# An attention, MLP and expert kernel: gated values on other engines, later routing sums, weights ahead of small tiles

## The chip, the cores and the metric

The kernel runs on one core of a Trainium2 chip. TensorE (PE in the profile) multiplies matrices, VectorE (DVE), ScalarE (ACT) and GpSimd (POOL) work element by element, SyncE (SP) issues most DMAs. Each engine runs its instructions in a fixed order and waits on semaphores for the others. The metric is the device time of one execution in microseconds (us); the kernel before took 972.35 us (median of three runs, 971.67 to 975.25).

## The reference, cut to what matters

```python
local = softmax(causal(q @ k.T / 8)) @ v               # 4 batches, 8 heads, 576 rows, 64 wide
mem   = (phi(q) @ M_prev) / (phi(q) @ z_prev + 1e-6)
x = g * mem + (1 - g) * local                          # 2304 tokens x 512
h = x @ w_in                                           # 512 -> 2048
x = (h * clip(h + 3, 0, 6) / 6) @ w_out                # 2048 -> 512
logits = x @ w_gate; e = argmax(logits)                # 8 experts, each token goes to one
out = p[e] * sigmoid((x @ w_output_gate)[e]) * (relu(x @ w1[e]) @ w2[e])
```

The MLP's output decides which expert each token goes to, so the expert stage starts with a sorting of the tokens ("routing") that can finish only when the MLP has.

## The kernel before, in words

Matrix products that need more precision than one pass gives are made of three: each operand is rounded to a shorter format (names ending in `H`) and the remainder is kept too (`L`), and HH, HL and LH products are added in PSUM.

**Attention** goes over 16 pairs of heads. For each pair, `scores` multiplies and VectorE takes the row minimum (`mn`, L343) while it copies the scores out of PSUM (`st`); `exp` on ScalarE gives `a`; `norm` on GpSimd divides by the sums (L365); `turn` transposes and `values` multiplies by v. A string of steps (`PROGRAM`) says in which order the steps of neighbouring pairs are written, and a scheduler then orders the instructions of each engine. Ahead of the first pair stand a few loads: q, k, the memory part's q (`qnt`), beta (`bt`), and the two gate matrices (`wg`, L409), which are rounded at once (`wgs`, L410 and L411) though they are used only after the MLP.

**The MLP** (`mlp`) works on blocks of 256 tokens and on two halves of the hidden width. In a block, each of eight units makes 128 hidden columns for 256 tokens (`hps`, L213), gates them (`g`, L216 on ScalarE and L217 on VectorE), rounds (`gH`, L95 on GpSimd) and takes the remainder (`gL`, L221 on GpSimd). The second product of a unit (`acc`, L182) is written two units later. After the second half's block, `end2` adds the first half's part (`row`, L528), makes the logits (`lg`) and, last, the gate factor (`gates`, L573 on).

Beside the last block, the expert that has most tokens so far is chosen, its weights are fetched (`st`) and split on ScalarE and VectorE (`wH` L641, `wL` L646), two tiles of its tokens are picked with one-hot matrices (`ohc`, L812) and gathered by GpSimd (`xg`, L659).

**The experts** take tiles of 128 tokens, 19 of them here. A tile is `hidden` (two halves of 512 columns, `ph`, 12 matmuls each), relu (`hs`, L693), transposes (`px`, L667), rounding and remainder (`hH`, `hL`), and `result` (`py`, L701, 24 matmuls). While a tile is computed, the weights of the next one are split again, and the ones after that are fetched chunk by chunk as `wL` frees a staging buffer. A fetch has a condition (`sw`): it moves no bytes where the next tile has the same expert. From here on the order of PE, DVE, ACT and POOL is as it is written (`manual_schedule`); SP's DMAs are ordered by the scheduler.

`route` writes the routing on VectorE in steps (`next(routing)`): counts, ranks and positions, one-hot matrices (`ohc`, `rh`), a product (`inv`, L908) that gives the token lists (`idx`), the expert of each tile and the condition (`ei`, `sw`, L901 and L902, from `c1` and `c2`), and last the lists of the small tiles (`inq`, `idq`, `esm`).

Four experts whose last tile has at most 32 tokens get no tile for them. These **small tiles** (`small`) run inside another tile, the host (tiles 4, 6, 9 and 11), one step after each of the host's groups of matmuls (`tick`): gather, transposes (`xT`), product (`ph`, L1038), relu (`hq`, L1043), transposes (`pt`, `hT`, L1047 and L1049), second product (`py`, L1056). Their weights (`sw` as a tile name: 8 chunks of 512 KB, L1020 and L1022) go through four buffers of their own. The expert numbers that SP needs for an address are read from `ei`, `sw` and `esm` by `value_load` (TENSOR_LOAD on SP).

Of the kernel before, what the change touches and what calls it, by code (L numbers as in the profile page):

```python
# [11 lines left out]
F32 = DT.float32  # L12
# [5 lines left out]
ALU = mybir.AluOpType  # L18
# [59 lines left out]
def f32(ap):  # L78
    return ap.bitcast(F32)
# [3 lines left out]
def tile_kernel(ctx, tc, qT, kT, qn, vx, z, beta, w_in, w_out, w_gates, w1, w2, out):  # L83
# [84 lines left out]
    def mlp(blocks, half_, end, begin=None):  # L168
# [24 lines left out]
        for n in blocks:  # L193
            xH = xs.tile([P, KD, TB], F32R, name="xH")
            xL = xs.tile([P, KD, TB], F32R, name="xL")
            o = n * TB % XB
            xn = xt[n * TB // XB][:, :, o : o + TB]
            for k in range(KD):
                copy(XH, xH[:, k], xn[:, k])
                ENG[XL].tensor_tensor(xL[:, k], xn[:, k], f32(xH[:, k]), op=ALU.subtract)  # L200
            if n == blocks[0]:
                yield
            if queue:
                second()
                follow()
                yield
            for m in range(HM):
                wH, wL = wts[half_][m]
                hps = ps_h.tile([P, 512], F32, name="hps", tag="h")[:, :TB]
                k = 0  # L210
                for kk in range(KD):
                    for ww, xx in ((wH, xH), (wH, xL), (wL, xH)):
                        PE.matmul(hps, lhsT=ww[:, kk * P : (kk + 1) * P], rhs=xx[:, kk], start=k == 0, stop=k == 3 * KD - 1)  # L213
                        k += 1
                g = gp.tile([P, TB], F32, name="g")
                ACT.activation(g, hps, AF.Relu, bias=half, scale=1.0 / 6.0)  # L216
                DVE.scalar_tensor_tensor(g, g, 1.0, hps, op0=ALU.min, op1=ALU.mult)  # L217
                gH = ghp.tile([P, TB], F32R, name="gH")
                gL = ghp.tile([P, TB], F32R, name="gL")
                copy(GH, gH, g)  # L220
                ENG[GL].tensor_tensor(gL, g, f32(gH), op=ALU.subtract)  # L221
                follow()
                yield
                if len(queue) >= (1 if m == 0 and n == NB - 1 else LAG):
                    second()
                    follow()
                    yield
                queue.append((n, m, gH, gL))
# [180 lines left out]
    SP.dma_start(wg, w_gates.rearrange("(k p) e -> p k e", p=P))  # L409
    ACT.copy(wgs[:, :, : 2 * E], wg)  # L410
    DVE.tensor_tensor(wgs[:, :, 2 * E :], wg, f32(wgs[:, :, : 2 * E]), op=ALU.subtract)  # L411
# [63 lines left out]
    for t in range(-1, len(pairs)):  # L475
        for x in PROGRAM.split():
            act(t, x)
    for _ in it:
        pass
# [266 lines left out]
    def flat(x):  # L746
        return x.rearrange("p a b -> p (a b)")
# [72 lines left out]
    def route():  # L820
# [16 lines left out]
        DVE.tensor_tensor(gtc, cnt.to_broadcast([P, E, NJ]), mid(io18, E), op=ALU.is_gt)  # L837
        yield
# [38 lines left out]

        c1, c2 = (r2.tile([P, NI, E], F32, name=x) for x in ("c1", "c2"))
        DVE.tensor_tensor(c1, mid(flat(base), NI), itl.to_broadcast([P, NI, E]), op=ALU.is_le)
        DVE.tensor_copy(tf, ti)  # L880
        DVE.tensor_tensor(c2, mid(flat(end), NI), itl.to_broadcast([P, NI, E]), op=ALU.is_le)
        gates = got["gates"]
        next(gates)
# [3 lines left out]
        DVE.tensor_tensor(c1, c1, c2, op=ALU.subtract)  # L887
# [3 lines left out]
        DVE.tensor_tensor(c1, c1, mid(io8, NI), op=ALU.mult)  # L891
# [4 lines left out]
        ef = r2.tile([P, NI + 1, 1], F32, name="ef")  # L896
        DVE.memset(ef[:, 0:1], 0.0)
        DVE.tensor_reduce(ef[:, 1 : NI + 1], c1, axis=AX.X, op=ALU.add)
        rh = r2.tile([P, NJ, 3, NI + NS], BF16, name="rh")
        DVE.tensor_tensor(rh[:, :, 0], mid(ion, NJ), tf.to_broadcast([P, NJ, NI + NS]), op=ALU.is_equal)  # L900
        DVE.tensor_copy(ei, flat(ef)[:, 1 : NI + 1])  # L901
        DVE.tensor_tensor(sw, flat(ef)[:, 1 : NI + 1], flat(ef)[:, 0:NI], op=ALU.not_equal)  # L902
# [12 lines left out]

        DVE.tensor_scalar(iv[:, 0], iv[:, 0], -1.0e6, 1.0e6, op0=ALU.mult, op1=ALU.add)
# [5 lines left out]
        DVE.tensor_copy(ivs, inv3[:, :, NI:])  # L922
        inq = ps_g.tile([P, 512], F32, name="inq", tag="pg")[:, : 3 * NS]
# [10 lines left out]
        c3 = r.tile([P, NS, E], F32, name="c3")  # L934
        DVE.tensor_tensor(c3, mid(flat(key), NS), ion[:, 1 : NS + 1].rearrange("p (n o) -> p n o", o=1).to_broadcast([P, NS, E]), op=ALU.is_equal)
        DVE.tensor_tensor(c3, c3, mid(io8, NS), op=ALU.mult)
        ef3 = r.tile([P, NS, 1], F32, name="ef3")
        DVE.tensor_reduce(ef3, c3, axis=AX.X, op=ALU.add)
        DVE.tensor_copy(esm, flat(ef3))
# [66 lines left out]
    def small(s):  # L1006
# [34 lines left out]
        yield  # L1041
        hq = smp.tile([P, FF // 4], F32, name="hq")
# [7 lines left out]
        for _ in range(9):  # L1050
            yield
# [26 lines left out]
    def tiles(i0, i1, w, xg, xn, xx):  # L1078
        nonlocal beside, smp
        for i in range(i0, i1):  # L1080
            if i + 1 in HOSTS and i + 1 < i1:
                ahead = small(HOSTS[i + 1])
                next(ahead)
# [7 lines left out]
            if more:  # L1091
                w.fetch(0, 1, 2, 3, 4, 5, 7, 6)
            high, low = (w.high, w.low) if more else (lambda *cs: None,) * 2

            hs, hh = hidden_out()
# [12 lines left out]
            ph = stepped(g, 2)  # L1108
            high(3)
# [110 lines left out]
```

## Time and profile before

| | |
|---|---|
| median of three runs | 972.35 us |
| the profiled execution | 975.48 us, of which the span from first to last instruction is 973.4 us |
| busy: PE, weight load, DVE, ACT, POOL | 94%, 74%, 64%, 53%, 38% of the span |
| mean granted TensorE clock | 0.978 of full speed |

The profile is of one execution. PE is the engine that is nearly always busy, so the time is read from the places where PE stands idle or runs at a lower clock, and from what ends each of those waits.

### The profile page before, as it was taken

To read this page: it belongs to the slowest core of one execution; us is meant where nothing else is said; L and a number is where in the kernel's file an instruction comes from. 1 tells how busy PE (TensorE), PEld (TensorE's weight loads), DVE (VectorE), ACT (ScalarE), POOL (GpSimd) and SP (SyncE) were. 2 spreads that over 40 slices of the span, in tenths; PEclk is the share of its full clock that TensorE was granted. 3 is DMA by queue.
4 is the path that set the end of the run, shared out by engine and by line. 5 is a ranking of instruction groups with operands and counts; after the bars stand their busy time and mean duration, and the time that the engine had idled before them with its cause. 6 is when DMAs were issued, how large, how long until landed. Compare 5 with 4: busy or idle time off the path is not lost. (4 is left out here: it accounts for less than half of the span.)

```text
span 973.4 us, 17053 instructions
## 1 busy us (share of the span) xinstructions
PE 915.6 (94%) x5733; PEld 721.7 (74%) x5733; DVE 627.7 (64%) x1511; ACT 519.3 (53%) x1084; POOL 370.5 (38%) x574
## 2 busy tenths in 40 slices
PE   5788889999999999899999999998997999999996
PEld 3445667777777778779988888887775777778785
DVE  6889996576556533686344444448766769668982
ACT  5677665565555454444222222223345768668883
POOL 2636556465555443245433333336021212112210
PEclk9989899999999999899999999999999999999998
DMA  5434432121212003443011111113223664633850
GB/s 181 139 112 146 131 100 74 52 86 52 78 54 90 14 23 109 130 131 108 1 45 44 44 44 45 44 44 138 80 77 120 218 250 176 208 131 119 311 205 23
DMA packets 49277, 101.69 MB, mean 104 GB/s; under 512 B 5341, under 2 KB 15581, under 8 KB 49184
## 3 DMA queue, kind: packets, MB, share of 16 engines
q1 hardware_dynamic: 45696, 89.74, 27.3%
q0 software_dynamic: 3488, 10.80, 3.3%
q8 instruction: 47, 0.77, 0.3%
q14 instruction: 46, 0.38, 0.1%
HBM read 136.66 MB, written 14.72 MB: 156 GB/s over the span
## 5 line engine op out<-in xcount | busy, mean ns | idle before, releaser
L646 DVE TENSOR_TENSOR wL<-st,wH 128x1024 fp32r<-128x1024 f32 x136 | 163.7, 1227 | 42.7 <-ACT wH L641 41.5
L95 POOL TENSOR_SCALAR gH<-g 128x256 fp32r<-128x256 f32 x144 | 65.5, 455 | 271.4 <-DVE g L217 213.5
L213 PE MATMUL hps<-xH,wH 128*128 128x256 f32 x576 | 167.3, 291 | 1.5 <-ACT xH L91 1.0
L213 PE MATMUL hps<-xL,wH 128*128 128x256 f32 x576 | 163.0, 283 | 2.4 <-DVE xL L200 2.4
L213 PE MATMUL hps<-xH,wL 128*128 128x256 f32 x576 | 161.7, 281 | 0.0
L365 POOL TENSOR_SCALAR a<-a,rs,omg 128x320 f32<-128x320 f32 (+4 forms) x160 | 128.1, 812 | 78.0 <-DVE rs L360 52.1
L217 DVE SCALAR_TENSOR_TENSOR g<-g,hps 128x256 f32<-128x256 f32 x144 | 60.0, 417 | 146.4 <-ACT g L216 146.4
L641 ACT CAST wH<-st 128x1024 fp32r<-128x1024 f32 x136 | 139.7, 1053 | 8.4 <-DMA st<-w 8.3
L216 ACT ACTIVATE g<-hps,half 128x256 f32<-128x256 f32 x144 | 68.1, 473 | 139.2 <-PE hps L213 116.0
L213 PEld LDWEIGHTS hps<-xH,wH 128*128 128x128 f32 x576 | 109.5, 191 | 18.3 <-issue 12.6
L221 POOL TENSOR_TENSOR gL<-g,gH 128x256 fp32r<-128x256 f32 x144 | 115.8, 804 | 11.7
L213 PEld LDWEIGHTS hps<-xL,wH 128*128 128x128 f32 x576 | 109.8, 191 | 8.4 <-DVE xL L200 3.4
L352 ACT ACTIVATE a<-st,mn 64x64 f32<-64x64 f32 (+4 forms) x160 | 88.4, 555 | 43.9 <-DVE mn L343 43.8
L213 PEld LDWEIGHTS hps<-xH,wL 128*128 128x128 f32 x576 | 109.8, 191 | 0.1
L182 PE MATMUL acc<-wH,gH 128*128 128x512 f32 x288 | 95.8, 414 | 0.2 <-POOL gH L95 0.2
L337 PE MATMUL pa<-kd,qd 64*128 64x64 f32 (+5 forms) x384 | 82.1, 470 | 13.8 <-DVE mn L343 8.7
L182 PE MATMUL acc<-wH,gL 128*128 128x512 f32 x288 | 91.6, 400 | 2.3 <-POOL gL L221 2.3
L182 PE MATMUL acc<-wL,gH 128*128 128x512 f32 x288 | 91.0, 398 | 0.0
L376 PE MATMUL pa<-ident,a 128*128 128x128 f32 (+1 forms) x480 | 75.3, 289 | 13.3 <-DVE mn L343 8.0
L376 PEld LDWEIGHTS pa<-ident,a 128*128 128x128 f32 (+1 forms) x480 | 55.6, 145 | 37.1 <-DVE mn L343 14.0
L708 POOL DMA_INDIRECT out<-ys,idxs x17 | 19.2, 1128 | 124.7 <-ACT ys L707 69.4
L182 PEld LDWEIGHTS acc<-wH,gL 128*128 128x128 f32 x288 | 54.3, 190 | 15.9 <-POOL gL L221 3.1
(239 smaller groups left out, 1720.8 us busy)
## 6 DMA issues: line engine op xcount, KB each, us to landing
st<-w SPq DMA_DIRECT2D x136, 512.0 KB
sw<-w SPq DMA_DIRECT2D x32, 512.0 KB
w<-w_in SPq DMA_DIRECT2D x16, 512.0 KB
w<-w_out SPq DMA_DIRECT2D x16, 512.0 KB
qnt<-qn SPq DMA_DIRECT2D x16, 320.0 KB
vt<-vx SPq DMA_DIRECT2D x16, 320.0 KB
x2d<-row SPq DMA_DIRECT2D x18, 258.0 KB
qd<-qT SPq DMA_DIRECT2D x16, 288.0 KB
```

The costliest lines, as they stand in the source:

```text
L95: POOL.tensor_scalar(out, x, 1.0, 1.0, op0=ALU.mult, op1=ALU.mult)
L182: PE.matmul(acc[t], lhsT=gg[:, t * P : (t + 1) * P], rhs=ww[:, 512:1024], start=m == 0 and first, stop=m == HM - 1 and last)
L213: PE.matmul(hps, lhsT=ww[:, kk * P : (kk + 1) * P], rhs=xx[:, kk], start=k == 0, stop=k == 3 * KD - 1)
L216: ACT.activation(g, hps, AF.Relu, bias=half, scale=1.0 / 6.0)
L217: DVE.scalar_tensor_tensor(g, g, 1.0, hps, op0=ALU.min, op1=ALU.mult)
L221: ENG[GL].tensor_tensor(gL, g, f32(gH), op=ALU.subtract)
L337: PE.matmul(pss[j][: QN[i], o : o + k1 - k0], lhsT=self.qd[r, QS[i] : QS[i] + QN[i]], rhs=self.kd[r, k0:k1], start=True, stop=True)
L352: ACT.activation(self.a[j][:m, o + D : o + D + n], self.st[j][i][:m, :n], AF.Exp, bias=self.mn[j][:m, i : i + 1], scale=-1.0, accum_out=se ...
L365: ENG[NORM[i]].tensor_scalar(av, av, r[:m, i], omg[:m, h : h + 1], op0=ALU.mult, op1=ALU.mult)
L376: PE.transpose(psa[:, off : off + QN[i]], self.a[j][: QN[i], QO[i] + c * P : QO[i] + (c + 1) * P], ident[: QN[i], : QN[i]])
L641: ACT.copy(self.H[c], stage[c])
L646: DVE.tensor_tensor(self.L[c], stage[c], f32(self.H[c]), op=ALU.subtract)
```

## The change

The change has six edits. In the MLP's last block of the second half, from the fourth unit on (`m >= 3`), `gH` is made on ScalarE and `gL` on VectorE. The load and split of `wg` are written after the attention loop. In `route`, the first step of `gates` comes earlier, the sums for `ei` and `sw` come after `idx`, and the sums for `esm` come before `inq` and end in a step of their own. In `small`, four steps are added before `hq` and three taken away after `hT`. In `tiles`, the small tile's first step (gather, `esm`, four fetches) comes after the next tile's weight fetch. In tile 2, two routing steps are written earlier than the tile's end.

```diff
+                near = half_ == 1 and n == NB - 1 and m >= 3
+                copy("A" if near else GH, gH, g)
+                ENG["D" if near else GL].tensor_tensor(gL, g, f32(gH), op=ALU.subtract)
...
-    SP.dma_start(wg, w_gates.rearrange("(k p) e -> p k e", p=P))
-    ACT.copy(wgs[:, :, : 2 * E], wg)
-    DVE.tensor_tensor(wgs[:, :, 2 * E :], wg, f32(wgs[:, :, : 2 * E]), op=ALU.subtract)
...
         for x in PROGRAM.split():
             act(t, x)
+    SP.dma_start(wg, w_gates.rearrange("(k p) e -> p k e", p=P))
+    ACT.copy(wgs[:, :, : 2 * E], wg)
+    DVE.tensor_tensor(wgs[:, :, 2 * E :], wg, f32(wgs[:, :, : 2 * E]), op=ALU.subtract)
...
         DVE.tensor_tensor(gtc, cnt.to_broadcast([P, E, NJ]), mid(io18, E), op=ALU.is_gt)
+        gates = got["gates"]
+        next(gates)
         yield
...
-        DVE.tensor_tensor(c1, mid(flat(base), NI), itl.to_broadcast([P, NI, E]), op=ALU.is_le)
         DVE.tensor_copy(tf, ti)
-        DVE.tensor_tensor(c2, mid(flat(end), NI), itl.to_broadcast([P, NI, E]), op=ALU.is_le)
-        gates = got["gates"]
-        next(gates)
         yield
...
         DVE.tensor_copy(idx, tok)
+        DVE.tensor_tensor(c1, mid(flat(base), NI), itl.to_broadcast([P, NI, E]), op=ALU.is_le)
+        DVE.tensor_tensor(c2, mid(flat(end), NI), itl.to_broadcast([P, NI, E]), op=ALU.is_le)
+        DVE.tensor_tensor(c1, c1, c2, op=ALU.subtract)
+        DVE.tensor_tensor(c1, c1, mid(io8, NI), op=ALU.mult)
+        ef = r2.tile([P, NI + 1, 1], F32, name="ef")
+        DVE.memset(ef[:, 0:1], 0.0)
+        DVE.tensor_reduce(ef[:, 1 : NI + 1], c1, axis=AX.X, op=ALU.add)
+        DVE.tensor_copy(ei, flat(ef)[:, 1 : NI + 1])
+        DVE.tensor_tensor(sw, flat(ef)[:, 1 : NI + 1], flat(ef)[:, 0:NI], op=ALU.not_equal)
...
         DVE.tensor_copy(ivs, inv3[:, :, NI:])
+        c3 = r.tile([P, NS, E], F32, name="c3")
...
+        DVE.tensor_copy(esm, flat(ef3))
+        yield
         inq = ps_g.tile([P, 512], F32, name="inq", tag="pg")[:, : 3 * NS]
...
         while len(ws) < 2 * KD:
             fetch()
         yield
+        for _ in range(4):
+            yield
         hq = smp.tile([P, FF // 4], F32, name="hq")
...
-        for _ in range(9):
+        for _ in range(6):
             yield
...
-            if i + 1 in HOSTS and i + 1 < i1:
-                ahead = small(HOSTS[i + 1])
-                next(ahead)
...
                 w.fetch(0, 1, 2, 3, 4, 5, 7, 6)
+            if i + 1 in HOSTS and i + 1 < i1:
+                ahead = small(HOSTS[i + 1])
+                next(ahead)
             high, low = (w.high, w.low) if more else (lambda *cs: None,) * 2
 
+            if i == 2:
+                next(routing)
...
             ph = stepped(g, 2)
+            if i == 2:
+                next(routing)
             high(3)
```

VectorE at the end of the MLP's last block, before (line numbers are those of the kernel before):

```order
L818 SCALAR_TENSOR_TENSOR id_5328<-iv_7789 128x1
L646 TENSOR_TENSOR wL_7917<-st,wH_7915 128x1024
L817 COPY iv_7835<-pi 128x2
L217 SCALAR_TENSOR_TENSOR g<-g,hps 128x256
L818 SCALAR_TENSOR_TENSOR id_5328<-iv_7835 128x1
L646 TENSOR_TENSOR wL_7921<-st,wH_7919 128x1024
L959 SCALAR_TENSOR_TENSOR esi_5337<-id_5328,esi 128x1
L646 TENSOR_TENSOR wL_7945<-st,wH_7943 128x1024
L217 SCALAR_TENSOR_TENSOR g<-g,hps 128x256
L646 TENSOR_TENSOR wL_7949<-st,wH_7947 128x1024
L672 TENSOR_TENSOR xgL<-px,xgH 128x512
```

The same place of the changed kernel, whose lines from here on stand two or more higher:

```order
L820 SCALAR_TENSOR_TENSOR id_5328<-iv_7789 128x1
L223 TENSOR_TENSOR gL<-g,gH 128x256
L217 SCALAR_TENSOR_TENSOR g<-g,hps 128x256
L819 COPY iv_7835<-pi 128x2
L648 TENSOR_TENSOR wL_7917<-st,wH_7915 128x1024
L820 SCALAR_TENSOR_TENSOR id_5328<-iv_7835 128x1
L223 TENSOR_TENSOR gL<-g,gH 128x256
L962 SCALAR_TENSOR_TENSOR esi_5337<-id_5328,esi 128x1
L648 TENSOR_TENSOR wL_7921<-st,wH_7919 128x1024
L217 SCALAR_TENSOR_TENSOR g<-g,hps 128x256
L648 TENSOR_TENSOR wL_7945<-st,wH_7943 128x1024
L223 TENSOR_TENSOR gL<-g,gH 128x256
```

Five remainders `gL` have come from GpSimd into VectorE's order; the last of them stands ahead of the last `wL`.

ScalarE in a host tile, before (`xT`, `hq` and `hT` are the small tile's):

```order
L707 ACTIVATE ys<-py,xg 128x512
L1033 COPY xT<-px 128x128
L1043 ACTIVATE hq<-ph 128x256
L1049 COPY hT<-pt 128x256
L641 CAST wH_8784<-st 128x1024
L641 CAST wH_8786<-st 128x1024
L693 ACTIVATE hs<-ph 128x512
L641 CAST wH_8793<-st 128x1024
```

The same place of the changed kernel:

```order
L709 ACTIVATE ys<-py,xg 128x512
L1036 COPY xT<-px 128x128
L643 CAST wH_8777<-st 128x1024
L643 CAST wH_8779<-st 128x1024
L695 ACTIVATE hs<-ph 128x512
L643 CAST wH_8786<-st 128x1024
L1048 ACTIVATE hq<-ph 128x256
L1112 CAST hH<-px 128x512
L1054 COPY hT<-pt 128x256
```

`hq` and `hT` have moved behind the host's relu `hs`.

SP's queue after the weight fetch of tile 3, before (`esm` is the small tile's expert, `sw<-w` its weights, `st<-w` a tile's weights):

```order
L636 DMA st<-w 128x2x512
L654 TENSOR_LOAD ei
L654 ISA x2
...
L1009 TENSOR_LOAD esm
L1009 ISA x2
L1020 ISA
L1020 DMA sw<-w 128x1024
...
L636 REGISTER_ALU x2
L636 ISA
L636 DMA st<-w 128x1024
```

The same place of the changed kernel, where tile 4's fetch ends and the small tile's begins:

```order
L638 DMA st<-w 128x2x512
L1012 TENSOR_LOAD esm
L1012 ISA x2
L1023 ISA
L1023 DMA sw<-w 128x1024
...
L656 TENSOR_LOAD ei
L656 ISA x2
L657 TENSOR_LOAD sw
L657 ISA x2
```

Before, eleven pairs of `ei` and `sw` loads, the wait for `esm` and the small tile's fetches stand ahead of tile 4's fetch; now that fetch stands ahead of them, and each tile's pair of loads stands right before its own fetch.

## Rows read from the trace of the kernel before

**Rows 1.** PE's waits, whole run: us in total, times, longest us

```profile
PE px L667 <- ACT hs L693: 7.7, 6, 3.8
```

**Rows 2.** Stretches: us, busy time of each engine, clock, DMA share, GB/s

```profile
676.00:686.00 10.00, 7.70 (x33) 6.08 (x32) 6.21 (x10) 3.35 (x5) 6.31 (x6) 0.83 0.69 254
710.00:720.00 10.00, 9.19 (x50) 7.04 (x50) 3.17 (x10) 1.94 (x4) 2.05 (x2) 0.83 0.24 67
720.00:735.00 15.00, 13.71 (x66) 10.80 (x66) 12.61 (x20) 11.16 (x14) 2.69 (x2) 1.00 0.12 36
735.00:755.00 20.00, 16.16 (x95) 11.77 (x94) 12.05 (x15) 11.25 (x15) 4.92 (x5) 0.91 0.44 156
800.00:820.00 20.00, 20.00 (x96) 16.14 (x95) 17.53 (x17) 17.95 (x25) 7.26 (x6) 1.00 0.65 239
```

**Rows 3.** Timeline of the start, ACT, DVE, PE: start us, us, instruction, idle before

```profile
9.23 0.24 ACT L410 CAST wgs<-wg 128x64 fp32r<-128x64 f32 x1 [2.68 <-DMA wg<-w_gates]
...
10.39 0.82 DVE L292 SCALAR_TENSOR_TENSOR phi<-qnt,phi 128x640 f32<-128x640 f32 x1
...
12.42 2.07 PE L337 MATMUL pa<-kd,qd 64*128 64x512 f32 x2 [4.63 <-DVE mn L343]
```

**Rows 4.** Timeline of the MLP's end, PE, POOL, DVE

```profile
681.50 1.22 PE L182 MATMUL acc<-wH,gL 128*128 128x512 f32 x2 [2.31 <-POOL gL L221]
685.39 0.39 PE L688 MATMUL ph<-wH,xgH 128*128 128x512 f32 x1
...
668.92 2.64 POOL L221 TENSOR_TENSOR gL<-g,gH 128x256 fp32r<-128x256 f32 x1
679.85 1.60 POOL L221 TENSOR_TENSOR gL<-g,gH 128x256 fp32r<-128x256 f32 x1
...
679.10 1.78 DVE L646 TENSOR_TENSOR wL<-st,wH 128x1024 fp32r<-128x1024 f32 x1
```

**Rows 5.** The page's costliest groups, VectorE's gate: busy us, mean ns | idle before

```profile
L217 DVE SCALAR_TENSOR_TENSOR g<-g,hps 128x256 f32<-128x256 f32 x144 | 60.0, 417 | 146.4 <-ACT g L216 146.4
```

**Rows 6.** Timeline of the routing, DVE, ACT, PE

```profile
703.79 0.35 DVE L879 TENSOR_TENSOR c<-base,itl 128x192 f32<-128x192 f32 x1
704.06 0.17 DVE L880 CAST tf<-ti 128x18 f32<-128x18 int32 x1
...
704.81 0.20 ACT L576 ACTIVATE so<-so 128x2 f32<-128x2 f32 x1 [8.00 <-DVE so L575]
...
710.81 0.85 PE L908 MATMUL inv<-rh,ohc 128*128 128x84 bf16 x18 [1.40 <-DVE rh L904]
```

**Rows 7.** Timeline of tile 3, PE, ACT, SP

```profile
733.47 0.17 PE L924 MATMUL inq<-ivs,four 128*128 128x12 bf16 x1 [1.29 <-DVE ivs L922]
741.77 0.66 PE L667 MATMUL px<-ident,hs 128*128 128x128 f32 x4 [3.84 <-ACT hs L693]
...
739.23 1.99 ACT L641 CAST wH<-st 128x1024 fp32r<-128x1024 f32 x2 [6.32 <-DMA st<-w]
...
736.64 2.08 SPq L1020 DMA_DIRECT2D sw<-w  x4
```

**Rows 8.** Timeline of host tile 6, PE; last row: ACT in host tile 4

```profile
789.72 0.39 PE L688 MATMUL ph<-wL,xgH 128*128 128x512 f32 x1
789.95 0.40 PE L688 MATMUL ph<-wH,xgL 128*128 128x512 f32 x1
791.11 0.66 PE L667 MATMUL px<-ident,hs 128*128 128x128 f32 x4 [0.76 <-ACT hs L693]
793.24 0.40 PE L701 MATMUL py<-wL,hH 128*128 128x512 f32 x1
793.91 0.50 PE L701 MATMUL py<-wH,hL 128*128 128x512 f32 x1 [0.28 <-DVE hL L1107]
...
755.02 0.39 ACT L1043 ACTIVATE hq<-ph 128x256 f32<-128x256 f32 x1 [2.30 <-PE ph L1038]
```

**Rows 9.** Stretch in which the first small tile's four fetches end

```profile
746.00:747.00 1.00, 1.00 (x8) 0.76 (x7) 0.80 (x1) 0.17 (x1) 0.00 (x0) 0.92 0.29 99
```

More of the change, by code (lines that the diff above doesn't have):

```diff
@@ L219, in mlp @@
                 gL = ghp.tile([P, TB], F32R, name="gL")
-                copy(GH, gH, g)
-                ENG[GL].tensor_tensor(gL, g, f32(gH), op=ALU.subtract)
+                near = half_ == 1 and n == NB - 1 and m >= 3
+                copy("A" if near else GH, gH, g)
+                ENG["D" if near else GL].tensor_tensor(gL, g, f32(gH), op=ALU.subtract)
                 follow()
@@ L876, in route @@
         DVE.tensor_copy(cf, ci)
-        c1, c2 = (r2.tile([P, NI, E], F32, name=x) for x in ("c1", "c2"))
-        DVE.tensor_tensor(c1, mid(flat(base), NI), itl.to_broadcast([P, NI, E]), op=ALU.is_le)
         DVE.tensor_copy(tf, ti)
-        DVE.tensor_tensor(c2, mid(flat(end), NI), itl.to_broadcast([P, NI, E]), op=ALU.is_le)
-        gates = got["gates"]
-        next(gates)
         yield
@@ L886, in route @@
         next(gates)
-        DVE.tensor_tensor(c1, c1, c2, op=ALU.subtract)
         next(gates)
@@ L890, in route @@
         next(gates)
-        DVE.tensor_tensor(c1, c1, mid(io8, NI), op=ALU.mult)
         next(gates)
@@ L895, in route @@
         yield
-        ef = r2.tile([P, NI + 1, 1], F32, name="ef")
-        DVE.memset(ef[:, 0:1], 0.0)
-        DVE.tensor_reduce(ef[:, 1 : NI + 1], c1, axis=AX.X, op=ALU.add)
         rh = r2.tile([P, NJ, 3, NI + NS], BF16, name="rh")
         DVE.tensor_tensor(rh[:, :, 0], mid(ion, NJ), tf.to_broadcast([P, NJ, NI + NS]), op=ALU.is_equal)
-        DVE.tensor_copy(ei, flat(ef)[:, 1 : NI + 1])
-        DVE.tensor_tensor(sw, flat(ef)[:, 1 : NI + 1], flat(ef)[:, 0:NI], op=ALU.not_equal)
         DVE.tensor_scalar(rh[:, :, 1], rh[:, :, 0], iop, None, op0=ALU.mult)
@@ L914, in route @@
         DVE.tensor_copy(idx, tok)
+        c1, c2 = (r2.tile([P, NI, E], F32, name=x) for x in ("c1", "c2"))
+        DVE.tensor_tensor(c1, mid(flat(base), NI), itl.to_broadcast([P, NI, E]), op=ALU.is_le)
[7 more added lines that the diff above has]
+        DVE.tensor_tensor(sw, flat(ef)[:, 1 : NI + 1], flat(ef)[:, 0:NI], op=ALU.not_equal)
         DVE.tensor_scalar(iv[:, 0], iv[:, 0], -1.0e6, 1.0e6, op0=ALU.mult, op1=ALU.add)
@@ L922, in route @@
         DVE.tensor_copy(ivs, inv3[:, :, NI:])
+        c3 = r.tile([P, NS, E], F32, name="c3")
+        DVE.tensor_tensor(c3, mid(flat(key), NS), ion[:, 1 : NS + 1].rearrange("p (n o) -> p n o", o=1).to_broadcast([P, NS, E]), op=ALU.is_equal)
+        DVE.tensor_tensor(c3, c3, mid(io8, NS), op=ALU.mult)
+        ef3 = r.tile([P, NS, 1], F32, name="ef3")
+        DVE.tensor_reduce(ef3, c3, axis=AX.X, op=ALU.add)
+        DVE.tensor_copy(esm, flat(ef3))
+        yield
         inq = ps_g.tile([P, 512], F32, name="inq", tag="pg")[:, : 3 * NS]
@@ L933, in route @@
         DVE.tensor_copy(idq, tks)
[L934 to L939, printed above, removed]
         yield
```

## The prediction

> **What bounds the kernel now.** I read the table of waits of PE first, because PE is busy for 94% of the span, then the table by stretches, then the timeline of each place where PE waits. The longest class of waits after the start is for the relu `hs`: 7.7 us in 6 waits, one of them 3.8 [rows 1]. The stretches [rows 2] show where PE has work to win back: in 800 to 820 it is busy for all of the 20.00 us at full clock, so an ordinary expert tile has nothing to give; in 676 to 686, 710 to 720 and 735 to 755 it is idle for 2.3, 0.8 and 3.8 us, and the mean clock is 0.83, 0.83 and 0.91. The clock has two levels (1.2 and 2.4 GHz), so 0.83 over 10 us is 3.4 us at the lower one and 0.91 over 20 us is 3.6 us; half of that is lost, 1.7, 1.7 and 1.8 us. So each of those waits costs more than its length. The start has one more long wait, 4.63 us [rows 3]. What the change can give is the sum over these places; all else is covered by a full PE.
>
> **The start.** ScalarE stands 2.68 us for the DMA of `wg` [rows 3], in front of the exponentials that VectorE needs, and VectorE's score minima, which free PE's banks, stand behind its part of `wgs`; PE's 4.63 us wait ends with them. With `wg` gone from here, ScalarE's next operand is `bt`, issued before `wg`; when it lands the trace does not show, only that ScalarE went on with it right after the `wgs` cast that starts at 9.23. So the gain is 2.7 at most and 0 at least; a loss would need ScalarE to be held longer by the fetches that now come earlier (`w_out` is cast before the first pair's exponentials end). The new order also puts `phi` (0.82 us) ahead of the first minimum, which cost nothing while it stood behind it. From 2.7 less 0.8 I take **1.8 us**. It is kept to the end if the attention's engines only wait for each other and nothing for a fixed time; the moved `wgs` pieces, 0.24 us each, then lie beside a full PE.
>
> **The MLP's last block.** PE waits 2.31 us for the remainder `gL`, which started late on GpSimd and took 1.60 us there; another took 2.64 us [rows 4]. With the lower clock after it that is 4.0 us. On ScalarE and VectorE neither wait exists for `gL`, but VectorE has no idle time here until its last weight remainder ends at 679.10 + 1.78 = 680.9 [rows 4], and five `gL` come on top. The trace shows none of this operation on VectorE; the gate of the same shape takes 0.42 us [rows 5], so five take 2.1. The first tile's `hidden` then waits for `xgL` behind that last remainder: 680.9 + 2.1 = 683.0, less some 0.4 that GpSimd no longer takes from VectorE by an estimate from the 1.78 us, against a start at 685.39 [rows 4]. That is 2.4 to 3.4 us; bounds are 0 (VectorE is the new limit all the way to the routing) and 4.0. I take **2.9 us**. The trace bears on this from another side: the remainder of 2.64 us on GpSimd ran while VectorE built its one-hot matrix. The Trainium skill ("SBUF — State Buffer", section "Who interferes with whom") says that a VectorE instruction with two SBUF inputs and a GpSimd one that reads SBUF exclude each other for a whole instruction, and the trace agrees with its 2.64. By that rule the five remainders on VectorE could still push back GpSimd's gather of the first tile, by up to 2.1 us, and the sum below would be 15.0 instead of 17.1.
>
> **The routing.** From the last `oh` to `inv` VectorE works without a break, and PE waits 1.40 us for it before `inv` [rows 6]. Four `c` sums leave that chain at 0.27 each (703.79 to 704.06 [rows 6]), and with the reduction and two casts for `ei` and `sw`, which I estimate at 0.4 from the same rows, 1.5 us. Against that, the first `gates` step now stands ahead of `hH` in ScalarE's order: `hH` and `hL` wait until VectorE has made `so`, some 0.8 us by the steps between. In return the output and the relu behind it no longer wait for `so` (8.00 us of ScalarE [rows 6]); that is PE time which the `inv` wait would take back. Net **0.65 us**, with -1.0 and 1.5 as ends. The 1.7 us of lower clock around 715 go or stay: the waits that remain before `inv`, about 1.9 us, lie between those that brought it (2.5 with the two ahead of it) and the 1.29 us before `inq`, after which the clock is 1.00 [rows 2, 7]. If they go, VectorE's sums for `ei`, now behind `idx`, delay the next `hL` by 0.8. Of 0 to 0.9 I take **0.4**. The Trainium skill ("TensorE: Matmul & The Clock Gate", Part 1) calls the slow clock the default that activity releases; by that rule any wait left here could bring it back, this term would be 0, and the sum 16.7.
>
> **Tile 3.** PE waits 1.29 us at `inq`, because `ivs` came after all weight remainders of tile 2, and 3.84 us for `hs`; ScalarE was held 6.32 us by the fetch of tile 4's weights [rows 7]. That fetch moves next to nothing: it stood in SP's queue behind the small tile's four fetches, which SP issued at 736.64 when `esm` was made, and ScalarE went on at 739.23. Now `ivs` and `esm` come at the start of tile 2, where VectorE waits, and the tile's fetch stands first, so both waits end: 1.3 + 3.8 + 1.8 of clock = 6.9. The seven small operations from `iq` to `idq` now stand inside tile 2 ahead of a weight remainder and `hL`; they come in all to about 1.4 us, of which half finds VectorE idle. **6.2 us**; ends are 0 and 6.9. The `ei` and `sw` loads now wait for sums behind `idx` and come some 3 us later, but SP has the rest of tile 1 for them.
>
> **The hosts.** `hq` waits 2.30 us for the small product on ScalarE [rows 8], and the host's own casts and `hs` stand behind it. PE pays 0.76 and 0.28 us in each host. From start to start it is 1.16 (789.95 to 791.11) and 0.67 (793.24 to 793.91), where matmuls without a wait stand 0.23 apart (789.72 to 789.95) [rows 8]: 1.83 - 0.46 = 1.4. Now `hq` comes behind `hs` and has its input by then, and `hT` waits for `pt` about 0.7 us in front of one cast that has as much slack. I take 1.3 each, four times: **5.2 us**, with 0 and 5.6 as ends.
>
> **The sum.** 1.8 + 2.9 + 0.65 + 0.4 + 6.2 + 5.2 = 17.15 us. The profiled execution took 975.48 us, so it would take 958.3. It was 3.1 us slower than the median of the runs, 972.35; from the median the sum gives 955.2, and I forecast **955**.
>
> **Rivals.** (1) *Tile 3's wait stays.* SP reaches tile 4's fetch late for another reason, such as the later `ei`; for it speaks that both loads now stand in the queue right before each fetch, against it that SP has 8 us and more. Without the 3.8 and 1.8 the time is 960.8. (2) *The early gains are not kept.* VectorE stays the limit from the MLP's end to the routing, and the start is absorbed by the attention. For it: VectorE's full order at the block's end. Without 1.8 and 2.9 it is 959.9. (3) *New waits in the old places.* The host tiles wait for `hT` instead of `hq`, the lower clock comes back in all three places, and the block's end stays. That gives back 5.2, 0.4, 1.8, 2.9 and, with `idq` in full in front of `hL`, 0.7 and the routing's 0.65: 966.9 at the start's full gain, some 968.5 without it. (4) *The small weights come late, and the kernel is slower.* Now the four fetches of a small tile stand behind the weights of the tile before its host. Before, they were issued at 736.64 and the traffic ended within 746 to 747 [rows 9], 10 us later. Now they can be issued when tile 3's last weight remainder frees its buffer, at the end of tile 2, about 734.5 on this time scale; they land by 744.5. PE needs them one tile of some 12.5 us (48 matmuls at 0.23, 12 transposes) and a few matmuls after 732, about 745.9. So there is 1.4 us to spare. If they were to land a further 10 us later, as behind eight fetches that really move bytes, each host waits 8.6 us, four of them 34, and the time is 989. The point from which this decides is 4.3 us of wait per host; tiles of the same expert, which move nothing, speak against it.
>
> **How the numbers follow.** The forecast has 0.66, rival 1 0.12, rival 2 0.14, rival 3 0.05, rival 4 0.03. What a measurement of this kernel can tell from no change is 0.5%, here 4.9 us, so faster means under 967.5. The forecast and rivals 1 and 2 lie there: 0.92. Rival 3 lies around that line: same, 0.05. Slower: 0.03. With the upper ends of all terms (2.7 + 4.0 + 1.5 + 0.9 + 6.9 + 5.6 = 21.6) the median is 950.8, and the start and the clock can be off by a little more; the range reaches from 948 to 964, so that it takes in rivals 1 and 2.
>
> **What would show it.** Right: no wait of `acc` for `gL` and a first `ph` about 3 us nearer to the last `hps`; no `inq` wait, no wait of ScalarE for `st` in tile 3, clock 1.00 there; no `px` wait for `hs` in the four hosts; PE's second group of scores about 2 us earlier. Wrong: PE waiting for `sw` in a host, `wH` still waiting for `st` in tile 3, or new waits of PE for `hL` in tiles 1 and 2 above 1 us. The forecast falls if two of the three terms above 2.5 us fail.

## The result and the profile after

The changed kernel took 960.42 us (median of four runs, 959.20 to 960.97) against 972.01 of the kernel before in the same comparison (four runs): ratio 0.9872, interval 0.9848 to 0.9895. A second comparison gave 960.66 against 973.28, ratio 0.9865 (0.9838 to 0.9893). By the medians the gain is 11.6 and 12.6 us; the forecast was 955, a gain of 17.15. The sign was right and about 5 us were missing.

The profiled execution after took 959.20 us, with a span of 957.3. First PE's stretches, at the places that answer to [rows 2] (columns as there):

```profile
671.00:681.00 10.00, 10.00 (x71) 8.44 (x70) 9.72 (x17) 5.96 (x11) 3.03 (x2) 1.00 0.64 237
...
704.00:714.00 10.00, 7.51 (x49) 5.53 (x49) 6.29 (x20) 1.22 (x3) 2.18 (x2) 1.00 0.34 108
714.00:729.00 15.00, 14.89 (x69) 11.06 (x68) 13.17 (x24) 12.58 (x17) 2.71 (x2) 1.00 0.12 36
729.00:749.00 20.00, 20.00 (x122) 15.12 (x121) 15.40 (x16) 15.48 (x22) 6.20 (x5) 1.00 0.68 244
```

The reader is to see that PE is now full in the MLP's last block (10.00 of 10.00, before 7.70; both stretches end just behind the first `ph`) and in tile 3 (20.00 of 20.00, before 16.16), in this execution all at full clock. Counted over the ten microseconds from the last `hps` on, the block has 9.56 where it had 7.70. Only the routing, 704 to 714, still has larger holes: 2.5 us idle. The table of PE's waits says the same. The class that was longest in the experts, `px` for `hs` [rows 1], has left its first twenty rows, and what is left from the last block on is small:

```profile
PE py L703 <- DVE hL L674: 1.4, 2, 0.8
...
PE inv L899 <- DVE rh L895: 1.1, 1, 1.1
...
PE pf L762 <- DVE ohb L824: 1.0, 1, 1.0
...
PE px L1034 <- DMA sx<-x2d,idr: 0.3, 1, 0.3
```

**The start**, timeline of ScalarE and PE, which answers to [rows 3]:

```profile
9.53 0.21 ACT L411 ACTIVATE gt<-bt 128x8 f32<-128x8 f32 x1 [3.38 <-DMA bt<-beta]
...
13.30 3.30 PE L339 MATMUL pa<-kd,qd 64*128 64x512 f32 x4 [5.37 <-DVE mn L345]
```

ScalarE's wait has only changed its name: it stands for `bt` now, to 9.53 instead of 9.23, and PE's long wait is 5.37 us instead of 4.63; its second group of scores starts at 13.30, before at 12.42.

**The MLP's end**, DVE, PE and ACT, which answers to [rows 4]:

```profile
678.23 0.42 DVE L223 TENSOR_TENSOR gL<-g,gH 128x256 fp32r<-128x256 f32 x1
678.56 1.22 DVE L648 TENSOR_TENSOR wL<-st,wH 128x1024 fp32r<-128x1024 f32 x1
...
679.73 0.40 PE L690 MATMUL ph<-wH,xgH 128*128 128x512 f32 x1
...
680.72 1.05 ACT L643 CAST wH<-st 128x1024 fp32r<-128x1024 f32 x1 [1.60 <-DMA st<-w]
...
684.79 1.05 ACT L643 CAST wH<-st 128x1024 fp32r<-128x1024 f32 x1 [0.70 <-DMA st<-w]
```

A remainder `gL` takes 0.42 us on VectorE, as the prediction bounded it from the gate's row, and no `acc` waits for it. The last weight remainder takes 1.22 us where it took 1.78. New are waits of ScalarE for the weights of the next tile, 1.60, 0.30 and 0.70 us. The kernel before had none behind its last `hps`.

**The routing**, ACT, DVE and PE, which answers to [rows 6]:

```profile
692.29 0.17 DVE L571 TENSOR_TENSOR oh<-t,mx 128x16 f32<-128x16 f32 x1
...
694.17 0.21 ACT L578 ACTIVATE so<-so 128x2 f32<-128x2 f32 x1 [2.33 <-DVE so L577]
694.28 0.57 ACT L673 CAST hH<-px 128x512 fp32r<-128x512 f32 x1
694.88 0.69 DVE L674 TENSOR_TENSOR hL<-px,hH 128x512 fp32r<-128x512 f32 x1 [0.74 <-ACT hH L673]
...
706.83 0.85 PE L899 MATMUL inv<-rh,ohc 128*128 128x84 bf16 x18 [1.07 <-DVE rh L895]
...
711.60 0.50 PE L703 MATMUL py<-wH,hL 128*128 128x512 f32 x1 [0.84 <-DVE hL L674]
```

`hH` is held behind `so`, VectorE waits 0.74 us for it, and `inv` is 14.54 us behind `oh`. In the trace before it was 14.74 (`oh` at 696.07).

**Tile 3**, PE and SP, which answers to [rows 7, 9]:

```profile
721.00 0.18 PE L933 MATMUL inq<-ivs,four 128*128 128x12 bf16 x1
...
730.46 2.10 SPq L1023 DMA_DIRECT2D sw<-w  x4
732.17 0.60 PE L669 MATMUL px<-ident,hs 128*128 128x128 f32 x4
```

Neither `inq` nor `px` waits. The small weights are issued at 730.46, and PE uses them at 741.93 without a wait. **A host**, ACT and PE, which answers to [rows 8]:

```profile
777.52 0.60 PE L669 MATMUL px<-ident,hs 128*128 128x128 f32 x4
...
777.82 0.39 ACT L1048 ACTIVATE hq<-ph 128x256 f32<-128x256 f32 x1
...
780.06 0.39 PE L703 MATMUL py<-wH,hL 128*128 128x512 f32 x1
```

`hq` comes behind `hs`, nothing waits for it, and both of PE's waits are gone.

### The profile page after: what moved, and what is told of

The parts are those of the page before. It is cut to its first block, busy times and chain, and to the rows that moved or that the text cites. A ratio compares the mean times of both kernels' runs of the same rounds, so it can differ in the third digit from the quotient of the medians.

```text
span 957.3 us, 17051 instructions
## 1 busy us (share of the span) xinstructions
PE 904.5 (94%) x5733; PEld 713.8 (75%) x5733; DVE 629.8 (66%) x1516; ACT 521.0 (54%) x1089; POOL 360.2 (38%) x564
## 5 line engine op out<-in xcount | busy, mean ns | idle before, releaser
L95 POOL TENSOR_SCALAR gH<-g 128x256 fp32r<-128x256 f32 x139 | 62.8, 452 | 270.2 <-DVE g L217 209.8
L213 PEld LDWEIGHTS hps<-xH,wH 128*128 128x128 f32 x576 | 108.8, 189 | 18.5 <-issue 12.6
L223 POOL TENSOR_TENSOR gL<-g,gH 128x256 fp32r<-128x256 f32 x139 | 107.6, 774 | 11.4
L339 PEld LDWEIGHTS pa<-kd,qd 64*128 64x128 f32 (+1 forms) x384 | 38.1, 192 | 35.7 <-DVE mn L345 16.3
```

Source lines behind the costliest of these rows:

```text
L95: POOL.tensor_scalar(out, x, 1.0, 1.0, op0=ALU.mult, op1=ALU.mult)
L223: ENG["D" if near else GL].tensor_tensor(gL, g, f32(gH), op=ALU.subtract)
L339: PE.matmul(pss[j][: QN[i], o : o + k1 - k0], lhsT=self.qd[r, QS[i] : QS[i] + QN[i]], rhs=self.kd[r, k0:k1], start=True, stop=True)
```

## The experiments

Each kernel ran beside the kernel before on the same chip. Of single executions I compare distances between landmarks of the timeline, since these say where a difference lies. Absolute times of late landmarks say less: in six profiles of kernels whose code is the same up to there (the result's and runs 5 to 9) the last `hps` starts anywhere between 674.70 and 677.35. Line numbers are each kernel's own; they differ by a few.

**1. The kernel before, again.** No edit.

> The kernel before, unchanged, for a second profile of it, because its profiled execution took 975.48 us and the median of its runs 972.0. Theory A (the excess of 3.5 us sits in a few places, which the prediction counted as gains): this profile is near 972, and shows the excess in the waits and the lower clock at the MLP's end, at 712 to 716 or in tile 3, so that the terms of the sum shrink by up to 3.5. Theory B (the excess is spread over attention and MLP, where no term stands): the landmarks up to the last MLP block come 1 to 3 us earlier, and the terms stay as they are.

Median 974.44, ratio 1.0004 (0.9988 to 1.0021); profiled 974.06 us. So an execution of 975 is an ordinary one: here the kernel before ran from 969.75 to 977.24. The same stretches as in [rows 2]:

```profile
676.00:686.00 10.00, 7.68 (x52) 6.30 (x50) 7.55 (x13) 4.07 (x6) 7.44 (x7) 1.00 0.64 202
710.00:720.00 10.00, 9.25 (x57) 7.03 (x57) 3.67 (x11) 3.51 (x5) 3.16 (x4) 1.00 0.26 66
...
735.00:755.00 20.00, 16.26 (x96) 11.90 (x95) 11.41 (x11) 11.64 (x16) 5.06 (x5) 0.91 0.54 178
```

The waits there are the same to 0.1 us, but the clock is 1.00 in the first two places, where it was 0.83. The lower clock after a wait comes in one execution and not in the next. From the last `hps` to the first `px` it takes 14.81 us with the lower clock and 13.32 without, from `inv` to tile 2's first `px` 12.79 and 11.27: 1.5 us each time. Theory A was right in kind. Two clock terms of the sum were luck of one execution; tile 3's, which came again, was not.

The profiles of the other runs bear this out. Where the block's wait for `gL` stands (the kernel before twice, runs 2 and 4), the ten microseconds from the last `hps` on had the lower clock in two of four executions, and in none of the ten where it is gone. In tile 3 it came in all six executions in which `px` waits 2.65 us or more for `hs`, and in none of the other eight. In the six microseconds behind `inv` it came in three of five executions with the old routing (the profile before, runs 2 and 4; not in runs 1 and 3) and in two of nine with the new one (runs 5 and 7).

**2. Only the start.**

```diff
-    SP.dma_start(wg, w_gates.rearrange("(k p) e -> p k e", p=P))
-    ACT.copy(wgs[:, :, : 2 * E], wg)
-    DVE.tensor_tensor(wgs[:, :, 2 * E :], wg, f32(wgs[:, :, : 2 * E]), op=ALU.subtract)
...
         for x in PROGRAM.split():
             act(t, x)
+    SP.dma_start(wg, w_gates.rearrange("(k p) e -> p k e", p=P))
+    ACT.copy(wgs[:, :, : 2 * E], wg)
+    DVE.tensor_tensor(wgs[:, :, 2 * E :], wg, f32(wgs[:, :, : 2 * E]), op=ALU.subtract)
```

> Only the load and split of wg moved behind the attention loop. By the prediction's term 1.8 us less than before: 970.2. By the trace of the changed kernel, in which beta lands as late as wg did and ScalarE waits 3.38 us for it: no change, 972.0, and PE's first long wait between 4.6 and 5.5 us. A third way: the score minimum, now behind phi and 0.9 us later, costs 1 us: 973.

Median 974.11, ratio 1.0009 (0.9991 to 1.0028): no gain that the runs show.

```profile
9.45 0.21 ACT L409 ACTIVATE gt<-bt 128x8 f32<-128x8 f32 x1 [2.66 <-DMA bt<-beta]
...
13.22 3.29 PE L337 MATMUL pa<-kd,qd 64*128 64x512 f32 x4 [5.31 <-DVE mn L343]
```

The second way holds: `bt` lands as late as `wg` did.

**3. Only the MLP's block.**

```diff
-                copy(GH, gH, g)
-                ENG[GL].tensor_tensor(gL, g, f32(gH), op=ALU.subtract)
+                near = half_ == 1 and n == NB - 1 and m >= 3
+                copy("A" if near else GH, gH, g)
+                ENG["D" if near else GL].tensor_tensor(gL, g, f32(gH), op=ALU.subtract)
```

> Only the last MLP block's gH on ScalarE and gL on VectorE from unit 4 on. By the prediction's term 2.9 us less: 969.1. By the two traces, in which the block's end came 3.8 us nearer to the last hps: 968.2. Rival (the gain meets VectorE and the weight fetches at the start of the routing and is eaten there): the first px of the experts is 3.8 us earlier, but the one-hot matrix oh only 2.5, and the total is 969.5 or more.

Median 972.66, ratio 0.9987 (0.9968 to 1.0006): 1.3 us by the ratio, with 0 inside the interval (3.1 us less to 0.6 more). The block itself gained what was forecast: from the last `hps` to the last `acc` it takes 4.27 us (before 8.34, again 6.86). But from the first `px` of the experts to `inv` it takes 20.63 us, before 19.41 in both traces. VectorE's rows on that way:

```profile
691.15 0.19 DVE L561 TENSOR_TENSOR lg<-pg,lg 128x32 f32<-128x32 f32 x1
...
692.51 0.69 DVE L673 TENSOR_TENSOR xgL<-px,xgH 128x512 fp32r<-128x512 f32 x1 [1.16 <-ACT xgH L672]
693.12 0.16 DVE L563 TENSOR_REDUCE mx<-lg 128x2 f32<-128x16 f32 x1
```

The scheduler now puts `xgL`, with its wait of 1.16 us, ahead of `mx`. In the kernel before `mx` stood first:

```profile
693.76 0.17 DVE L562 TENSOR_REDUCE mx<-lg 128x2 f32<-128x16 f32 x1
...
695.06 0.69 DVE L672 TENSOR_TENSOR xgL<-px,xgH 128x512 fp32r<-128x512 f32 x1 [0.92 <-ACT xgH L671]
```

In all 1.2 us are given back in the rival's place, ahead of `oh`: from `px` to `lg` it takes 2.87 us (before 2.13), where VectorE has weight remainders behind ScalarE's late casts, and from `lg` to `oh` 3.03 (before 2.54), where the order is new. ScalarE's waits for `st` behind the last `hps` are 1.05, 0.30 and 1.20 us here; that they are what costs the first 0.7 us is argued from the order and not shown by a run of its own.

**4. Only the hosts.**

```diff
         yield
+        for _ in range(4):
+            yield
         hq = smp.tile([P, FF // 4], F32, name="hq")
...
-        for _ in range(9):
+        for _ in range(6):
```

> Only the small tile's steps: four before hq, three fewer after hT. By the prediction 1.3 us in each of four hosts, 5.2 less: 966.8. By the two traces 5.0: 967.0. Rival (the gain of the hosts comes only together with the earlier esm and the new fetch order, since hT or the second product then waits): at least half of it is missing, 969.5 or more, with new waits of PE in the hosts.

Median 967.72, ratio 0.9934 (0.9909 to 0.9959): 6.4 us by the ratio, 4 to 9 by its interval. From tile 3's second `px` to tile 18's first it takes 205.4 us, before 210.8, and neither wait of PE stands in a host. The four hosts need no other edit, and the rival falls.

**5. The changed kernel, again**, beside three that undo one edit each.

> The changed kernel once more, beside the three that undo one of its edits. If the single edits add up, the sum of start 0, MLP block 1.3 and hosts 6.4 (measured alone) and the prediction's 6.2 for tile 3 gives 13.9 us below the kernel before on the same chip, ratio 0.986; the first comparison had 0.987. If the prediction's own sum of 17.15 holds against the kernel before at 974.6, the ratio is 0.982. The profile should again have no wait of PE for hs in the experts.

Ratio 0.9865, as told above: the prediction's sum (0.982) lies outside the interval. The expected sum (0.986) lies inside, but it took tile 3's 6.2 us from the prediction and left the routing out; with the 4.3 to 5.0 that run 9 gives for tile 3 it is 0.987 to 0.988, inside as well. The profile, 963.02 us, differs from the first in one place of weight, the stretch around `inv`:

```profile
706.00:716.00 10.00, 8.36 (x46) 6.44 (x45) 6.77 (x22) 1.18 (x2) 2.18 (x2) 0.83 0.34 108
```

Here the changed kernel has the lower clock in the routing. `px` waits once for `hs`, 0.6 us in the first tile, which was expected not to be, and once 1.1 us for a small tile's gather (`sx`), where the first profile had 0.3.

**6. The first gate step late.**

```diff
         DVE.tensor_tensor(gtc, ...)
-        gates = got["gates"]
-        next(gates)
         yield
...
         DVE.tensor_copy(tf, ti)
+        gates = got["gates"]
+        next(gates)
         yield
```

> The changed kernel with the first step of the gate factor back in its old place, behind tf. Theory A (the early step holds hH and so VectorE's chain, as in the trace: hH starts 2.0 us after oh instead of -0.1): inv comes 0.8 to 1.1 us earlier, the total 0.5 to 1.0 lower. Theory B (the early step pays, because ScalarE no longer waits 8.00 us for so in front of ys and hs): PE's 0.85 us wait for hs in tile 1 is back and eats the gain, the total the same within 0.5.

Median 959.44, 1.2 below the changed kernel of the same comparison (0.5 by the ratios); ratio to before 0.9860 (0.9832 to 0.9888).

```profile
692.07 0.58 ACT L673 CAST hH<-px 128x512 fp32r<-128x512 f32 x1
...
692.59 0.18 DVE L571 TENSOR_TENSOR oh<-t,mx 128x16 f32<-128x16 f32 x1
...
702.13 0.66 PE L669 MATMUL px<-ident,hs 128*128 128x128 f32 x4 [0.34 <-ACT hs L695]
...
706.22 0.85 PE L899 MATMUL inv<-rh,ohc 128*128 128x84 bf16 x18 [1.07 <-DVE rh L895]
```

`hH` is free of `so`, `oh` to `inv` takes 13.63 us instead of 14.54, and PE's wait for `hs` comes back with 0.34 only. By the timeline theory A holds (0.9 us); the medians point the same way, but their intervals overlap.

**7. The small tile's first step ahead of the weight fetch.**

```diff
+            if i + 1 in HOSTS and i + 1 < i1:
+                ahead = small(HOSTS[i + 1])
+                next(ahead)
             if i in HOSTS:
...
                 w.fetch(0, 1, 2, 3, 4, 5, 7, 6)
-            if i + 1 in HOSTS and i + 1 < i1:
-                ahead = small(HOSTS[i + 1])
-                next(ahead)
```

> The changed kernel with the small tile's first step (gather, esm, four fetches) again written ahead of the next tile's weight fetch. Theory A (the order in SP's queue is what ended the wait in tile 3): the wait of px for hs in tile 3 comes back, +3.8 to +5.6 us. Theory B (the wait came from the late esm alone, which is now made at the start of tile 2, so that SP finds it ready): no wait, the same within 0.5 us.

Median 960.14, ratio 0.9869 (0.9841 to 0.9897): no change, and no wait at `inq` or for `hs` in tile 3. SP's queue, the small weights ahead of the tile's:

```profile
723.46 1.94 SPq L1023 DMA_DIRECT2D sw<-w  x4
...
727.00 9.31 SPq L638 DMA_DIRECT2D st<-w  x12
```

**8. No earlier routing steps in tile 2.**

```diff
-            if i == 2:
-                next(routing)
             hs, hh = hidden_out()
...
-            if i == 2:
-                next(routing)
             high(3)
```

> The changed kernel without the two earlier routing steps in tile 2, so esm, inq and idq are made at the end of that tile again; the fetch order stays. Theory A (the order in SP's queue ended tile 3's wait): only the wait for ivs at inq comes back, +1.3 us, with the lower clock after it up to +3.1. Theory B (the late esm was the cause): the small tile's fetches are issued as late as before, and either tile 3 waits again for hs (+3.8 to +5.6), or host tile 4 waits for the small weights, by 1 us or more.

Median 961.88, ratio 0.9885 (0.9857 to 0.9913), 1.2 above the changed kernel. PE:

```profile
729.93 0.17 PE L933 MATMUL inq<-ivs,four 128*128 128x12 bf16 x1 [1.29 <-DVE ivs L924]
...
734.21 0.60 PE L669 MATMUL px<-ident,hs 128*128 128x128 f32 x4
```

Only the 1.29 us at `inq` is back, at full clock. Run 7 confirms its theory B, run 8 its theory A, and the two together say that each edit alone suffices for `px`.

**9. Both undone.** The edits of 7 and 8 in one kernel.

> The changed kernel with both of tile 3's edits undone: the small tile's first step ahead of the tile's weight fetch, and no routing step earlier in tile 2. Undone singly, the one changed nothing and the other brought back only the 1.3 us at inq. Theory A (either edit alone ends the wait for hs, because SP's queue is held only when the late esm stands ahead of the fetch): now the wait of px for hs in tile 3 is back at about 3.8 us, with the lower clock up to 1.8, and the total is 5 to 7 us above the changed kernel, 966 to 968. Theory B (something else of the change ended it): no wait for hs, at most 962.5.

Median 964.98, ratio 0.9916 (0.9887 to 0.9944). That is 4.3 above the changed kernel's 960.66, which stood in another comparison, and 5.0 by the two ratios; from tile 2's first `px` to tile 3's second it takes 21.8 us, in the changed kernel 16.4.

```profile
730.91 1.95 SPq L1023 DMA_DIRECT2D sw<-w  x4
...
733.28 8.50 SPq L638 DMA_DIRECT2D st<-w  x8
733.37 1.99 ACT L643 CAST wH<-st 128x1024 fp32r<-128x1024 f32 x2 [5.17 <-DMA st<-w]
...
735.91 0.91 PE L669 MATMUL px<-ident,hs 128*128 128x128 f32 x4 [2.65 <-ACT hs L695]
```

The chain of the prediction is back link by link: `esm` late, the small weights at 730.91, the tile's fetch behind them, ScalarE 5.17 us for it, PE 2.65 us, and the lower clock after it (0.91 over the 20 us from 730.6). That wait is shorter than the 3.84 of before, and the total lies 1 us under what was expected; the cause of tile 3's wait is shown.

**10. Three units instead of five** (on top of run 6).

```diff
-                near = half_ == 1 and n == NB - 1 and m >= 3
+                near = half_ == 1 and n == NB - 1 and m >= 5
```

> The changed kernel with the first gate step late and with ScalarE and VectorE taking gH and gL from unit 6 on (m >= 5), three units instead of five. In VectorE's order the two steps mx and t of the logits then stand ahead of xgL again, as in the kernel before. Theory A (this order costs the block's gain on the way to the routing): from the first px of the experts to inv it takes 19.4 us or less instead of 19.5 to 20.4, lg to oh 2.8 instead of 3.2, and the total is 0.5 to 1.0 below the kernel with gates late, 958.5. Theory B (the two gL that go back to GpSimd are late again): PE waits for gL at the block's end, by 0.5 us or more, and the total is not lower.

Median 958.16, ratio 0.9844 (0.9813 to 0.9876). `mx` stands ahead of `xgL` again, `pf` waits 0.4 us instead of 1.1, and the first `px` to `inv` takes 18.46 us instead of run 6's 19.53; 0.7 of that lies between `lg` and `oh`, where the order differs. No wait for `gL` came back. The timeline agrees with theory A; the total alone would not tell it.

**11. Beta first** (on top of run 6).

```diff
+    SP.dma_start(bt, beta.rearrange("(o h) -> o h", o=1).to_broadcast([P, H]))
     pairs[0].load()
-    SP.dma_start(bt, beta.rearrange("(o h) -> o h", o=1).to_broadcast([P, H]))
```

> The changed kernel with the first gate step late and with the load of beta as SP's first DMA, 1.9 us earlier. Theory A (ScalarE's wait at the start is the DMA of beta): gt starts before 8 us instead of at 9.53, and PE's second group of scores 1.5 to 1.9 us before 13.30. If the attention keeps that, the first hps (47.9) and the total are 1.5 lower; if it is absorbed there, the first hps is the same within 0.5 and the total the same. Theory B (beta is late for another reason, such as many small packets that the larger loads hold back): gt starts after 9 us all the same.

Median 956.42, ratio 0.9830 (0.9797 to 0.9863), the lowest median of all.

```profile
0.80 0.40 SPq L409 DMA_DIRECT2D bt<-beta  x1
...
3.78 0.21 ACT L411 ACTIVATE gt<-bt 128x8 f32<-128x8 f32 x1 [1.70 <-DMA bt<-beta]
...
11.12 5.21 PE L339 MATMUL pa<-kd,qd 64*128 64x512 f32 x9 [2.00 <-DVE mn L345]
...
43.51 0.50 PE L213 MATMUL hps<-xH,wH 128*128 128x256 f32 x2
...
681.60 1.05 ACT L643 CAST wH<-st 128x1024 fp32r<-128x1024 f32 x1 [2.53 <-DMA st<-w]
...
684.00 0.28 PE L551 MATMUL pg<-x2H,wgs 128*32 128x256 f32 x1 [2.51 <-DVE x2L L544]
```

`bt` is used 5.94 us earlier than in run 6 (9.72 there; 1.5 or more was expected), PE's second group comes at 11.12 instead of 13.49, and the first `hps` at 43.51 instead of 47.91. So up to there the attention does not absorb the start; why 2.4 us at the second group become 4.4 was not settled. In this pair of executions 2.9 of the 4.4 us are left at the last `hps` and 1.5 at `inv`. In between PE now waits 2.51 us for `x2L` (the remainder of the MLP's output), which VectorE makes behind ScalarE, and ScalarE stands 2.53 us for a weight chunk; run 6 has no such wait of PE. The total is 3.0 below run 6, which stood in another comparison, and 1.7 below run 10 of the same one; the intervals overlap.

**12. All three.** The edits of 6, 10 and 11 in one kernel.

> The first gate step late, gH and gL moved from unit 6 on, and the load of beta first, in one kernel. If both places gain as hoped 957.5; if the start is absorbed 958.5; if neither pays the 959.4 of the kernel with gates late.

Median 957.62, ratio 0.9831 (0.9802 to 0.9860). Not lower than run 11. Its first `hps` is nearly as early (44.15), its last turn of the attention three us later than run 11's (373.77 against 370.72); why was not settled. PE again waits for `x2L` at the block's end, 1.61 us. Run 10 differs from this kernel in the place of beta alone, and its median is 0.5 higher, with overlapping intervals. So what an early beta gives at the first `hps` is seen twice, and that it reaches the total is not shown.

## Why the prediction came out as it did

The time came out 5 us above the forecast and inside its range. The two terms that carry most of the gain were right in mechanism; the start and the routing were not, and the block was in part, as the table shows. Each kernel has two profiles; of the kernel before the first had the lower clock in the block and the routing, of the changed kernel the second in the routing.

| step, from landmark to landmark | predicted | before, and run 1 | after, and run 5 | by an edit done or undone alone |
|---|---|---|---|---|
| start: PE's second group at | -1.8 | 12.42, 12.57 | 13.30, 13.34 | no gain (run 2) |
| MLP block: last `hps` to first `px` | -2.9 | 14.81, 13.32 | 11.40, 11.51 | -1.3, 0 not excluded (run 3) |
| routing and clock: first `px` to tile 2's | -1.05 | 32.20, 30.68 | 32.78, 33.23 | +0.9 for the gate step (run 6) |
| tile 3: tile 2's first `px` to tile 3's second | -6.2 | 23.0, 22.9 | 16.4, 16.4 | -4.3 to -5.0 (run 9) |
| hosts: from there to tile 18's first `px` | -5.2 | 210.8, 210.7 | 205.8, 206.6 | -6.4, within 4 to 9 (run 4) |

**Tile 3 and the hosts were right**, in mechanism and size: -6.6 and -5.0 by the timeline of the first two profiles, -6.5 and -4.1 by the second two. They are nearly the whole gain. The prediction named SP's queue as the cause of tile 3's wait; what it did not see is that the two edits there do the same work twice. Either of them (fetch first, or `esm` early) frees the queue. With the fetch first, the earlier routing steps earn only the 1.3 us at `inq`; with `esm` early, the fetch order earns nothing that the runs show.

**The start failed.** The step was "ScalarE's next operand is `bt`, issued before `wg`; when it lands the trace does not show", and of the bounds 0 and 2.7 I took the upper one, less the price of `phi`. Rows for the other bound existed in the trace before: `bt` was issued only 0.48 us ahead of `wg`, by the same queue.

```profile
2.67 0.43 SPq L408 DMA_DIRECT2D bt<-beta  x1
3.15 0.43 SPq L409 DMA_DIRECT2D wg<-w_gates  x1
```

Run 11 shows that the DMA itself can land within 3 us; issued fifth, behind loads of 288 and 320 KB, it needs 6.9. `phi` ahead of the first minimum did cost 0.7 to 0.9 us at PE's second group, as was feared, and the 2.7 us that were to pay for it never came; at the first `hps` 0.4 to 0.5 of that is left (47.86 and 47.91, before 47.40 and 47.48).

**The MLP's block was right in place and half kept.** VectorE had the room: `gL` takes 0.42 us, the last remainder ends at 679.78, and the first `ph` starts at 679.73. What failed is the step that a gain at the block's end arrives at the routing, which the prediction doubted only in its lower bound and in rival 2. There 1.2 us went back, 0.5 in the scheduler's new order (`xgL` ahead of `mx`) and 0.7 ahead of it, where VectorE stands behind ScalarE's waits for weights. The rule cited from the Trainium skill ("SBUF — State Buffer", section "Who interferes with whom") would have had GpSimd's gather pushed back by up to 2.1 us. The trace shows the first gather 1.19 us ahead of the last `hps`, before 1.60, and the second 0.94 us behind it, before 1.29. So at most 0.4 us of that price was paid; the shorter `wL` (1.22 for 1.78 us) fits its other side, since GpSimd no longer works there.

**The routing had the wrong sign.** The c sums left the chain and gave 1.1 us (14.73 to 13.63 from `oh` to `inv`, run 6; predicted 1.5). The early gate step cost 0.9 (predicted 0.8). But the return I booked for it, "PE time which the `inv` wait would take back", was all but absent: late, it costs 0.34 at `px`. The sums for `ei` behind `idx` delay `hL` and give PE a wait of 0.84 us, which I had foreseen but charged only to one case. And the block's 1.2 us appear in this stretch. Together +0.6 against a trace with the lower clock and +2.1 against one without it, where -1.05 was forecast. The 0.4 us for the clock rested on waits of 2.5 us that bring the lower clock and 1.29 us that do not. The profiles do not keep to that: in run 1 the same 2.5 us were followed by full clock, and in run 5 waits of 0.57 us for `hL` and 1.07 before `inv` by the lower one, where the result's profile has the same two waits and full clock. In run 5's execution the term was 0.

**The base.** The sum counted lower clock as a gain in two places (up to 1.7 us in the block, 0.4 in the routing), because one profiled execution showed it there. Run 1 shows that it is not always there. The medians differ by 11.6 and 12.6 us; the profiled pair, of which the first lay 3.5 above its median and the second 1.2 below its own, by 16.3; the second pair, runs 1 and 5, by 11.0. That the first pair comes so near to the 17.15 of the sum is luck.

Of the rivals, numbers 1 (960.8) and 2 (959.9) gave the measured time. Number 1 did so by chance: tile 3's wait is gone. Number 2 was half right: a good part of the block's gain is lost on the way to the routing, as it said, but the start was not absorbed, there was no gain to absorb. Numbers 3 and 4 fell: no wait for `hT` in the hosts, none for `sw`.

## What to carry to other kernels

When a wait ends with a transfer, look for the next transfer on that engine and ask when it would have landed; being there when the engine came to it says nothing, and here a transfer issued 0.48 us earlier in the same queue landed about as late. Before you add the gains of several edits, ask of each pair whether either would end the same wait alone, and follow a gain to the next shared point (here from the block to the token lists) before you book it. Take a second profile of the old kernel, and of the new one, before you put a lower clock into a sum.

## What was not expected of the hardware

The same waits, to 0.1 us, were followed by the lower clock in one execution and not in another (0.83 and 1.00 in 676 to 686). The mean granted clock of one kernel ran from 0.976 to 0.991 within one comparison and its time from 969.75 to 977.24. The mean is no measure of time by itself: in the comparison of runs 9 to 12 the kernel before took 971.09 us at 0.974 and 976.53 at 0.980. In the run with only the hosts changed, the profiled execution had 0.970, and part of its lower clock lay in the first 30 us, where PE waits anyway:

```profile
0.00:30.00 30.00, 17.10 (x48) 9.20 (x48) 17.53 (x60) 14.52 (x36) 10.47 (x30) 0.70 0.56 174
```

The profile before has PE busy for 17.11 us there at 1.00, and the first `hps` comes at 47.40 in that one and 47.60 in this one.

And the load of beta, a broadcast of 8 numbers to 128 partitions, landed 6.9 us after its issue as fifth load of the start, and within 3.0 us as the first.
